# Pooled attention and a two-layer network on one core: the last quarter of group 0's output product is placed among group 1's first hidden products, and the sums of VectorE and GpSimd are re-ordered

## The chip, the core and the metric

The kernel runs on one core of one Trainium2 chip. The metric is device time in microseconds (us), from one launch to its end. The kernel before was timed in 8 runs: median 286.16 us, from 285.38 to 286.41. One further execution was recorded by the hardware profiler, and every duration below is from that one.

## What is computed

Inputs are q, k and v with 8 batches, 8 heads, 576 positions and a head size of 64, and two weight matrices w_in (512 x 2048) and w_out (2048 x 512), all float32. The reference, cut to its core:

```python
k_p = k.reshape(B, H, Sp, 8, D).mean(axis=3)        # 576 rows -> 72
v_p = v.reshape(B, H, Sp, 8, D).mean(axis=3)
scores = scale * np.matmul(q, k_p.transpose(0, 1, 3, 2))
attn = np.exp(scores - np.max(scores, axis=-1, keepdims=True))
attn = attn / (np.sum(attn, axis=-1, keepdims=True) + 1e-09)
x = np.matmul(attn, v_p)                            # -> 4608 tokens x 512
h = x @ w_in
out = (h - np.tanh(h)) @ w_out                      # 4608 x 512
```

## The kernel before

**Groups.** The 4608 tokens are worked in nine groups of 512: groups 0 to 7 are the first 512 positions of one batch each, group 8 is what is left of all batches. For each group there is a hidden product (16 tiles of 128 hidden units, 4 matmuls each), then tanh on ScalarE and the subtraction h - tanh(h) on VectorE into a tile Gt, then an output product with w_out.

**Group 0 is different from the others.** Its output product is a plain one: four token blocks (tb 0 to 3) by four quarters of the hidden units (qd 0 to 3). A step `mlp_o(0, tb, qd)` (matmuls at L593) is four matmuls of 128x512. The quarters are taken in the order of `W2_ORDER`, hidden tiles 0-3, 8-11, 4-7 and 12-15, because w_out (the tile w2b) is loaded in such pieces, by GpSimd's DMA queue, with a cast to 16 bits (`load_w2`, L742). Groups 1 to 8 use seven products of half size instead of eight (L665). These need sums of the quarters of w_out, made once: `w_sum` (L648) into w2s, on VectorE and on GpSimd, and a negated part on ScalarE (L1015).

**Order.** The kernel is scheduled by hand (`manual_schedule`): every engine and every DMA queue takes its instructions strictly in the order in which the program text issues them, and waits where one of them has to wait. What follows in the text behind a waiting instruction of the same engine waits too. `after(a, b)` adds a wait by hand.

**The stretch that the change rewrites** lies between group 0's hidden product and group 1's output product. In the order of the text:

- The loop over hidden tiles 5 to 15 of group 0 (L951), matmuls at L564, subtraction at L577, PSUM banks 0 to 4 in turn.
- `pool_k(1)`: the sums of eight neighbouring rows of k of batch 1. First sum on GpSimd (L247), two loads of w_out (tiles 4-5 and 6-7), second sum on GpSimd (L252), the load of tiles 12-15, last sum on VectorE into kd (L259). Then two `w_sum` pieces on GpSimd, which wait for kd.
- SP's queue: the load of k of batch 2 (`load_k(2)`), which is made to wait for `w2_dmas[3]`, the load of tiles 6-7; then v and, a little later, q of batch 2.
- A loop over 16 steps u (L974), one `mlp_o` each. Between the steps stand batch 1's attention: turning k (L328) and q (L216) on TensorE by a product with the identity, the casts of q on ScalarE (L967, L992), scores (L374) and exp (L389, L406), the sums of v on VectorE (`pool_v(1)`, L270 to L309, in one piece of five tiles), the product with v (L463) and its division (L480, L481), and the turn of the result (L542, L549) into xT, group 1's input. On VectorE stand the `w_sum` pieces besides. The last quarter is steps 12 to 15; after it ScalarE copies each block out (L601) and SP stores it (L681).
- `pool_k(2)`, all three sums on GpSimd, `pool_v(2)` on GpSimd, and one last `w_sum` on VectorE.
- Group 1 (loop over g): seven `h_pair` steps (L608, eight matmuls into two PSUM banks, tanh L621 over both, subtraction L622), whose bank pairs start at 2, 0, 4, 6, 0, 2, 4; two `h_one`; then the seven products, among which stand scores and attention of batch 2 (L422, L448). During p 2 to 4 ScalarE casts q of batch 2 and SP turns it by DMA transposes (L202, L207); SP turns kd of batch 2 (L350), GpSimd places it (`k_place`, L360 to L362), SP spreads v (L293 to L295) and loads k, v and q of batch 3. In the products, SP turns group 2's input by DMA transposes (L527).

A pair of banks can be written again when the subtraction of its `h_pair` has read it:

```python
t2 = TS[:, 2 * ts : 2 * ts + 2, :]
nc.scalar.activation(out=t2, in_=PS[:, b0 : b0 + 2, :], func=ACT.Tanh)
nc.vector.tensor_sub(out=Gt[:, p, :, :], in0=PS[:, b0 : b0 + 2, :], in1=t2)
```

The softmax here doesn't subtract the row's maximum and nothing guards it: scores larger than these inputs give would overflow.

## Time and profile before

| what | us |
|---|---|
| median of 8 runs | 286.16 |
| the profiled execution: its own time | 286.41 |
| its span from first to last instruction | 284.7 |
| TensorE busy | 276.3 |
| VectorE busy | 223.5 |
| ScalarE busy | 157.8 |
| GpSimd busy | 115.1 |
| group 0's hidden product ends | 33.71 |
| group 1's first `h_pair` starts | 54.49 |
| group 1's seven products start | 68.32 |
| group 2's first `h_pair` starts | 84.15 |

The span and the 1.7 us around it make the execution's own time. TensorE is busy for 97% of the span, so it is read by its gaps: the list of waits names each gap and the engine or DMA that ended it. The chain of waits is the chain of work that ended last, followed back from the end of the span; a piece "PE PS L608 x72" in it is 72 matmuls of line 608 one after the other. The granted TensorE clock is full speed from the first slices to the last but one.

### The profile page before, as it was taken

What the parts mean: (1) busy time and instruction counts of PE and PEld (TensorE: products, weight loads), DVE (VectorE), ACT (ScalarE), POOL (GpSimd) and SP (SyncE); (2) the same over time, 40 slices, a digit from 0 to 9 for tenths busy, and PEclk for the clock granted to TensorE, in tenths of its full rate; (3) what the DMA queues carried; (4) which work ended last, traced back from release to release, by engine and by line L of the source; (5) the groups of instructions that cost most, each with busy time, mean ns of one, the idle gap of its engine ahead of it and who ended that gap; (6) DMA issues with size and microseconds to landing.
All of it is one profiled execution on the core that took longest, in us unless ns stands there. A gap on an engine that the chain in (4) does not pass through costs nothing.

```text
span 284.7 us, 5465 instructions
## 1 busy us (share of the span) xinstructions
PE 276.3 (97%) x2156; PEld 180.0 (63%) x2156; DVE 223.5 (78%) x338; ACT 157.8 (55%) x212; POOL 115.1 (40%) x124
## 2 busy tenths in 40 slices
PE   7999989999989999999999999999999999999994
PEld 3454445645874489548954795479547964884583
DVE  6568787989965998599959985998599839946983
ACT  4737567696527571867186708680868156215510
POOL 8600743693398019900990099109910110010000
PEclk9999999999999999999999999999999999999998
DMA  7999998974999894889588966897550440012014
GB/s 248 231 212 275 288 217 230 324 206 94 351 207 184 233 336 88 136 276 335 103 107 273 353 117 115 267 323 145 110 166 0 69 163 0 2 67 83 0 37 113
DMA packets 67253, 50.41 MB, mean 177 GB/s; under 512 B 42652, under 2 KB 56476, under 8 KB 67228
## 3 DMA queue, kind: packets, MB, share of 16 engines
q1 hardware_dynamic: 57724, 36.04, 50.5%
q0 software_dynamic: 6784, 12.06, 17.2%
q10 hardware_dynamic: 2720, 1.97, 2.4%
q8 instruction: 17, 0.28, 0.4%
q14 instruction: 8, 0.07, 0.1%
HBM read 36.70 MB, written 9.44 MB: 162 GB/s over the span
## 4 chain that ended last, share of the span: by engine, by line
PE 91%; DMA 4%; ACT 1%; DVE 1%; issue 1%; SPq 0%; ACTq 0%
PE PS L608 39%; PE PS L665 33%; PE PS L564 5%; PE PS L593 5%; PE PS L422 3%; PE PS L448 3%; DMA xT<-x_sb 2%; DMA k_raw<-in_k_dram 2%; PE PS L463 1%; PE PS L374 1%; ACT qT L132 0%; PE PS L844 0%; PE PS L905 0%; PE PS L216 0%; PE PS L755 0%
## 5 line engine op out<-in xcount | busy, mean ns | idle before, releaser
L608 PE MATMUL PS<-xT,w1b 128*128 128x512 bf16 (+1 forms) x504 | 98.1, 355 | 0.7 <-DMA xT<-x_sb 0.7
L622 DVE TENSOR_TENSOR Gt<-PS,TS 128x1024 bf16<-128x1024 f32 x56 | 68.4, 1221 | 33.2 <-ACT TS L621 33.1
L608 PEld LDWEIGHTS <-w1b 128*128 128x128 f16 x576 | 56.2, 98 | 53.7 <-DMA xT<-x_sb 1.0
L621 ACT ACTIVATE TS<-PS 128x1024 f32<-128x1024 f32 x56 | 57.3, 1024 | 31.0 <-PE PS L608 28.5
L709 POOL TENSOR_TENSOR m<-O,m 128x512 f32<-128x512 f32 x6 | 7.6, 1260 | 76.9 <-ACT m L707 76.9
L665 PE MATMUL PS<-w2s,Dg 128*128 128x256 f16 x256 | 30.2, 272 | 0.0
L247 POOL TENSOR_TENSOR k_raw<-k_raw 128x512 f32<-128x512 f32 (+2 forms) x13 | 21.5, 1672 | 19.1 <-DMA k_raw<-in_k_dram 19.1
L443 ACT ACTIVATE E<-PS 72x1024 bf16<-72x1024 f32 (+1 forms) x30 | 26.1, 929 | 4.0 <-PE PS L422 3.7
L665 PEld LDWEIGHTS <-Gt 128*128 128x128 bf16 x256 | 23.5, 98 | 6.8 <-issue 2.3
L665 PEld LDWEIGHTS <-P 128*128 128x128 bf16 x256 | 24.6, 98 | 3.0
L665 PEld LDWEIGHTS <-Dg 128*128 128x128 bf16 x256 | 24.6, 98 | 2.8
L630 DVE TENSOR_TENSOR P<-Gt 128x1024 bf16<-128x1024 bf16 x32 | 22.0, 687 | 0.6
L716 ACT COPY m<-PS 128x512 f32<-128x512 f32 x8 | 4.7, 586 | 29.6 <-PE PS L665 29.6
L681 POOL DMA_DIRECT2D out_dram<-O x14 | 7.7, 552 | 31.7 <-DVE O L719 29.5
L640 DVE TENSOR_TENSOR Dg<-Gt 128x1024 bf16<-128x1024 bf16 x32 | 20.4, 684 | 0.0
L270 POOL TENSOR_TENSOR v_raw<-v_raw 128x512 f32<-128x512 f32 (+1 forms) x12 | 18.2, 1536 | 0.0
L499 DVE TENSOR_TENSOR x_sb<-PS,rden 128x512 bf16<-128x512 f32 x24 | 16.6, 692 | 0.8
L665 PE MATMUL PS<-w2s,Gt 128*128 128x256 f16 x128 | 16.4, 273 | 0.0
L665 PE MATMUL PS<-w2b,P 128*128 128x256 f16 x128 | 16.3, 273 | 0.0
L665 PE MATMUL PS<-w2b,Gt 128*128 128x256 f16 x128 | 16.3, 272 | 0.0
L665 PE MATMUL PS<-w2s,Q 128*128 128x256 f16 x128 | 16.3, 272 | 0.0
L1090 ACT COPY O<-PS 128x512 f32<-128x512 f32 x7 | 4.1, 586 | 21.9 <-PE PS L665 21.9
(120 smaller groups left out, 405.7 us busy)
## 6 DMA issues: line engine op xcount, KB each, us to landing
k_raw<-in_k_dram SPq DMA_DIRECT2D x7, 1024.0 KB, 6.0
q_raw<-in_q_dram SPq DMA_DIRECT2D x7, 1024.0 KB, 11.3
v_raw<-in_v_dram SPq DMA_DIRECT2D x7, 1024.0 KB, 8.8
out_dram<-O POOLq DMA_DIRECT2D x14, 512.0 KB, 3.8
w1b<-in_moe_w_in_dram POOLq DMA_DIRECT2D x4, 512.0 KB, 14.1
w2b<-in_moe_w_out_dram POOLq DMA_DIRECT2D x3, 512.0 KB, 23.2
out_dram<-O SPq DMA_DIRECT2D x2, 512.0 KB, 7.0
k_raw<-in_k_dram SPq DMA_DIRECT2D x7, 128.0 KB, 6.0
```

Of the source, the lines that this page charges most:

```text
L247: eng.tensor_tensor(out=r[:, ta:tb, 0:4, :], in0=r[:, ta:tb, 0:4, :], in1=r[:, ta:tb, 4:8, :], op=ALU.add)
L270: eng.tensor_tensor(out=r[:, ta:tb, 0:4, :], in0=r[:, ta:tb, 0:4, :], in1=r[:, ta:tb, 4:8, :], op=ALU.add)
L443: nc.scalar.activation(out=e, in_=ps, func=ACT.Exp, scale=SCALE)
L499: nc.vector.tensor_tensor(out=x_sb[:, :, :, :], in0=ps[:, :, :, 0:D], in1=rden[:, :, :, :].to_broadcast([128, 2, 4, D]), op=ALU.mult,)
L564: nc.tensor.matmul(h_tiles[i][:, :], lhsT=w1b[:, fb, i * 128 : (i + 1) * 128], rhs=xT[g][:, :, fb, :], start=(fb == 0), stop=(fb == NFB - 1),)
L593: nc.tensor.matmul(o_ps[:, :], lhsT=gts[i][:, tb * 128 : (tb + 1) * 128], rhs=w2b[:, i, :], start=(i == 0), stop=(i == NHID - 1),)
L608: nc.tensor.matmul(dst[:, t0 * 128 : t1 * 128], lhsT=w1b[:, fb, i * 128 : (i + 1) * 128], rhs=x[:, t0:t1, fb, :], start=(fb == 0), stop=(f ...
L621: nc.scalar.activation(out=t2, in_=PS[:, b0 : b0 + 2, :], func=ACT.Tanh)
L622: nc.vector.tensor_sub(out=Gt[:, p, :, :], in0=PS[:, b0 : b0 + 2, :], in1=t2)
L630: nc.vector.tensor_tensor(out=P[:, a:b, :], in0=Gt[:, a:b, 0, :], in1=Gt[:, a:b, 1, :], op=ALU.add)
L640: return nc.vector.tensor_tensor(out=Dg[:, a:b, :, :], in0=Gt[:, a:b, :, 0:HT], in1=Gt[:, a:b, :, HT:TG], op=ALU.subtract,)
L665: nc.tensor.matmul(part(g, bk, tt), lhsT=lhs(k, slice(tt * 128, (tt + 1) * 128)), rhs=rhs[:, k, :], start=(first and k == 0 and (tt == 0 o ...
```

## The change

- In group 0's loop the sums of the fifth tile of v of batch 1 are made after hidden tile 9 (`pool_v1(NM, NT)`: four instructions on VectorE); the banks of the loop are i % 5 throughout. The load of v of batch 1 is in two halves.
- `pool_k(1)` issues no loads. Behind it on GpSimd's queue stand the two `w_sum` pieces that wait for kd, then one load of w_out's tiles 4-7. The load of tiles 12-15 stands later and is made to wait for the first load of k of batch 2, which in turn waits for `w2_dmas[2]`, now the load of tiles 4-7.
- The 16 steps are written out. Twelve of them (quarters 0 to 2) stay ahead of group 1; attention of batch 1 lies among them, with both halves of the division in one pair of instructions (L499, L500 in the new file) and the sums of v in pieces. Group 0's four PSUM tiles are banks 1, 2, 3 and 0; attention uses banks 4 to 7.
- `pool_k(2)`: first sums on GpSimd, second and last sum on VectorE, where they stand ahead of group 1's subtractions. `pool_v(2)`, two `w_sum` pieces and `k_place(2)` follow on GpSimd.
- Group 1's bank pairs start at 6, 4, 6, 4, 6, 4, 2. Ahead of p 4 stands `rest_of_group_0`: casts and DMA transposes of q of batch 2, the four steps of the last quarter with their copies and stores, three `w_sum` pieces and a sum for group 1 on VectorE, the loads of batch 3 and the spread of v on GpSimd's queue.

The engines' instruction streams otherwise hold the same work: TensorE has the same number of matmuls before and after.

```diff
@@ -237,7 +237,7 @@
     def halves(n, b):
         return ((0, n),) if b < 2 else ((0, n // 2), (n // 2, n))
 
-    def pool_k(b, eng, t0=0, t1=NT, mid=(), last=None, dep2=None):
+    def pool_k(b, eng, t0=0, t1=NT, last=None, second=None):
         r = k_raw[b % 2].rearrange("p t (j d) -> p t j d", d=D)[:, t0:t1, :, :]
         if b not in kdups:
             kdups[b] = work.tile([128, NT, 2, D], BF16, name="kd", tag="kd", bufs=1)
@@ -247,15 +247,9 @@
             eng.tensor_tensor(
                 out=r[:, ta:tb, 0:4, :], in0=r[:, ta:tb, 0:4, :], in1=r[:, ta:tb, 4:8, :], op=ALU.add
             )
-        for i, m in mid[0:2]:
-            load_w2(i, m)
-        second = eng.tensor_tensor(
+        (second or eng).tensor_tensor(
             out=r[:, :, 0:2, :], in0=r[:, :, 0:2, :], in1=r[:, :, 2:4, :], op=ALU.add
         )
-        if dep2 is not None:
-            after([second], dep2)
-        for i, m in mid[2:]:
-            load_w2(i, m)
         kd_done = (last or eng).tensor_tensor(
             out=kd,
             in0=r[:, :, 0:1, :].to_broadcast([128, n, 2, D]),
@@ -273,12 +267,6 @@
         eng.tensor_tensor(
             out=r[:, :, 0:2, :], in0=r[:, :, 0:2, :], in1=r[:, :, 2:4, :], op=ALU.add
         )
-        if b < 2:
-            eng.tensor_tensor(
-                out=r[:, :, 0, :], in0=r[:, :, 0, :], in1=r[:, :, 1, :], op=ALU.add
-            )
-            v_main(VB[b % 2], r[:, :, 0:1, :], eng, 0, NM)
-            return v_left(VB[b % 2], r[:, NM, 0:1, :], eng)
         if b < 4:
             eng.memset(VB[b % 2][0:G, 0:H, D:D1], float(POOL))
         vps[b] = work.tile([128, NT, D], BF16, name="vp", tag="vp", bufs=1)
@@ -286,17 +274,30 @@
             out=vps[b][:, :, :], in0=r[:, :, 0, :], in1=r[:, :, 1, :], op=ALU.add
         )
 
+    def pool_v1(ta, tb):
+        r = v_raw[1].rearrange("p t (j d) -> p t j d", d=D)
+        for n in (4, 2, 1):
+            nc.vector.tensor_tensor(
+                out=r[:, ta:tb, 0:n, :],
+                in0=r[:, ta:tb, 0:n, :],
+                in1=r[:, ta:tb, n : 2 * n, :],
+                op=ALU.add,
+            )
+        if ta == NM:
+            return v_left(VB[1], r[:, NM, 0:1, :], nc.vector)
+        return v_main(VB[1], r[:, :, 0:1, :], nc.vector, ta, tb)
+
     vps = {}
 
-    def v_spread(b):
+    def v_spread(b, eng=nc.sync):
         vp, vb = vps.pop(b), VB[b % 2]
-        nc.sync.dma_start(out=vb[0:G, 0:H:2, 0:D], in_=vp[0:G, 0:NM, :])
-        nc.sync.dma_start(out=vb[0 : 128 - G, 1:H:2, 0:D], in_=vp[G:128, 0:NM, :])
-        nc.sync.dma_start(out=vb[128 - G : G, 1:H:2, 0:D], in_=vp[0 : NM * LO, NM, :])
+        eng.dma_start(out=vb[0:G, 0:H:2, 0:D], in_=vp[0:G, 0:NM, :])
+        eng.dma_start(out=vb[0 : 128 - G, 1:H:2, 0:D], in_=vp[G:128, 0:NM, :])
+        eng.dma_start(out=vb[128 - G : G, 1:H:2, 0:D], in_=vp[0 : NM * LO, NM, :])
 
     def v_main(vb, vs, eng, t0, t1):
         n = t1 - t0
-        eng.tensor_tensor(
+        return eng.tensor_tensor(
             out=vb[:, 2 * t0 : 2 * t1, 0:D].rearrange("p (t s) d -> p t s d", s=2),
             in0=vs[:, t0:t1, :, :].to_broadcast([128, n, 2, D]),
             in1=mask[:, 2 * t0 : 2 * t1, :]
@@ -583,13 +584,12 @@
 
     o_tiles = {}
 
-    def mlp_o(g, tb, qd, gts, pool=None, k0=0, k1=4):
+    def mlp_o(g, tb, qd, gts):
         if qd == 0:
-            p, tag = pool or (ps_o, "o_ps")
-            o_tiles[tb] = p.tile([128, DM], FP32, name="o_ps", tag=tag)
+            o_tiles[tb] = bank((1, 2, 3, 0)[tb], [128, DM])
         o_ps = o_tiles[tb]
         i0 = W2_ORDER[qd]
-        for i in range(i0 + k0, i0 + k1):
+        for i in range(i0, i0 + 4):
             nc.tensor.matmul(
                 o_ps[:, :],
                 lhsT=gts[i][:, tb * 128 : (tb + 1) * 128],
@@ -941,7 +941,8 @@
     ps_h.n = ps_o.n = 0
     nc.scalar.copy(out=q_bf[:QT, R, :, :], in_=t0[:QT, :, R, :])
     load_q(1, False)
-    load_main(v_pairs, v_raw[1], 1, 0, NM)
+    load_main(v_pairs, v_raw[1], 1, 0, 2)
+    load_main(v_pairs, v_raw[1], 1, 2, 4)
     load_q_tail(1, q_raws[1], nc.scalar)
     for i in range(5):
         mlp_h_mms(0, i, 2, 4)
@@ -949,108 +950,132 @@
 
 
     for i in range(5, NHID):
-        mlp_h(0, i, gts, bank((0, 1, 2, 3, 4, 0, 1, 2, 3, 4, 2)[i - 5], [128, TG]))
+        mlp_h(0, i, gts, bank(i % 5, [128, TG]))
         if i == 7:
             q_pe_tail(0)
         if i == 9:
             scores_tail(0)
+        if i == 9:
+            pool_v1(NM, NT)
         if i == 11:
             ps_a.n = 0
             av(0, 4, ps_any, True)
             x_dma_transpose(0, 2)
-    kd1 = pool_k(1, nc.gpsimd, mid=((4, 2), (6, 2), (12, 4)), last=nc.vector)
-    after([w_sum(w2s[:, 3, :, :], b21, b11, ALU.subtract, nc.gpsimd, k, k + 2) for k in (0, 2)], kd1)
-    after(load_k(2), w2_dmas[3])
-    load_v(2)
-
-    def q1_cast(t, h):
+    def q1_cast(h):
         nc.scalar.copy(
             out=q_bf[:, 0:R, h : h + 4, :].rearrange("p j h d -> p h j d"),
-            in_=t[:, h : h + 4, 0:R, :],
-        )
-
-    o_pools = [(ps_o, "o_ps"), (ps_o, "o_ps"), (ps_h, "hT_ps"), (ps_h, "hT_ps")]
-    pend = []
-    for u in range(16):
-        qd, tb = u // 4, u % 4
-        if u == 8:
-            scores_wide(1, (3,))
-            scores_ends(1)
-        if qd == 2:
-            for t2 in (2 * (tb % 2), 2 * (tb % 2) + 1):
-                mlp_o(0, t2, qd, gts, o_pools[t2], tb // 2 * 2, tb // 2 * 2 + 2)
-        else:
-            mlp_o(0, tb, qd, gts, o_pools[tb])
-        if u == 0:
-            q1 = q_raws.pop(1)
-            q1_cast(q1, 0)
-        if u == 3:
-            k_transpose(1, ps_any, (nc.vector.tensor_copy, nc.vector.tensor_copy))
-        if u == 4:
-            q_pe_transpose(1, (0, 1), "act")
-            q1_cast(q1, 4)
-            nc.scalar.copy(out=q_bf[:QT, R, :, :], in_=q1[:QT, :, R, :])
-            load_q(2)
-            w_sum(w2s[:, 1, :, :], b11, b12, ALU.add, k1=4)
-            w_sum(w2s[:, 0, :, :], b11, b22, ALU.add, k1=4)
-            w_sum(w2s[:, 2, :, :], b21, b22, ALU.add, k1=4)
-            w_sum(b12, b22, b12, ALU.subtract, k1=4)
-            v1_done = pool_v(1, nc.vector)
-            after(
-                [
-                    w_sum(w2s[:, 3, :, :], b21, b11, ALU.subtract, nc.gpsimd, k, k + 2)
-                    for k in (4, 6)
-                ],
-                v1_done,
-            )
-            w_sum(w2s[:, 1, :, :], b11, b12, ALU.add, k0=4)
-        if u in (5, 6):
-            q_pe_transpose(1, (u - 3,), "act")
-        if 5 <= u <= 7:
-            scores_wide(1, (u - 5,))
-        if u == 6:
-            q_pe_tail(1)
-        if u in (9, 11):
-            n = (u - 9) // 2
-            nc.scalar.mul(
-                out=w2s[:, 4, 4 * n : 4 * n + 4, :], in_=b22[:, 4 * n : 4 * n + 4, :], mul=-1.0
-            )
-        if 11 <= u <= 14:
-            x_pe_transpose(1, *pend.pop(0))
-        if 9 <= u <= 12:
-            pend.append((u - 9, av(1, u - 9, ps_any, False)))
-        if u == 13:
-            w_sum(w2s[:, 0, :, :], b11, b22, ALU.add, k0=4)
-            sums = w_sum(w2s[:, 2, :, :], b21, b22, ALU.add, k0=4)
-        if u == 15:
-            ps_a.n = 0
-            av(1, 4, ps_any, True)
-    pool_k(2, nc.gpsimd, dep2=sums)
+            in_=q1[:, h : h + 4, 0:R, :],
+        )
+
+    def negated(n):
+        nc.scalar.mul(
+            out=w2s[:, 4, 4 * n : 4 * n + 4, :], in_=b22[:, 4 * n : 4 * n + 4, :], mul=-1.0
+        )
+
+    def turn1(blk):
+        x_pe_transpose(1, blk, x_pairs[1, blk // 2][:, blk % 2])
+
+    ps_a = Banks(4, 5, 6, 7)
+    q1 = q_raws.pop(1)
+    kd1 = pool_k(1, nc.gpsimd, last=nc.vector)
+    after([w_sum(w2s[:, 3, :, :], b21, b11, ALU.subtract, nc.gpsimd, k, k + 2) for k in (0, 2)], kd1)
+    load_w2(4, 4)
+    w_sum(w2s[:, 1, :, :], b11, b12, ALU.add, k1=4)
+    mlp_o(0, 0, 0, gts)
+    q1_cast(0)
+    q1_cast(4)
+    nc.scalar.copy(out=q_bf[:QT, R, :, :], in_=q1[:QT, :, R, :])
+    mlp_o(0, 1, 0, gts)
+    mlp_o(0, 2, 0, gts)
+    k_transpose(1, ps_any, (nc.vector.tensor_copy, nc.vector.tensor_copy))
+    w_sum(w2s[:, 0, :, :], b11, b22, ALU.add, k1=4)
+    w_sum(w2s[:, 2, :, :], b21, b22, ALU.add, k1=4)
+    mlp_o(0, 3, 0, gts)
+    mlp_o(0, 0, 1, gts)
+    q_pe_transpose(1, (0, 1), "act")
+    pool_v1(0, 2)
+    mlp_o(0, 1, 1, gts)
+    scores_wide(1, (0,))
+    q_pe_transpose(1, (2,), "act")
+    w_sum(b12, b22, b12, ALU.subtract, k1=4)
+    pool_v1(2, 4)
+    mlp_o(0, 2, 1, gts)
+    scores_wide(1, (1,))
+    q_pe_transpose(1, (3,), "act")
+    q_pe_tail(1)
+    mlp_o(0, 3, 1, gts)
+    scores_wide(1, (2, 3))
+    scores_ends(1)
+    negated(0)
+    w_sum(w2s[:, 1, :, :], b11, b12, ALU.add, k0=4)
+    mlp_o(0, 0, 2, gts)
+    ps_a.n = 0
+    k2 = load_k(2)
+    after(k2, w2_dmas[2])
+    load_v(2)
+    load_q(2)
+    load_w2(12, 4)
+    after([w2_dmas[3]], k2[0])
+    av(1, 0, ps_any, True)
+    av(1, 1, ps_any, True)
+    mlp_o(0, 1, 2, gts)
+    turn1(0)
+    mlp_o(0, 2, 2, gts)
+    turn1(1)
+    av(1, 2, ps_any, True)
+    av(1, 3, ps_any, True)
+    mlp_o(0, 3, 2, gts)
+    turn1(2)
+    turn1(3)
+    av(1, 4, ps_any, True)
+    pool_k(2, nc.gpsimd, last=nc.vector, second=nc.vector)
+    x_pairs.pop((1, 0))
+    x_pairs.pop((1, 1))
+    k_dma_transpose(2)
+    x_dma_transpose(1, 2)
     pool_v(2, nc.gpsimd)
-    w_sum(b12, b22, b12, ALU.subtract, k0=4)
+    for k in (4, 6):
+        w_sum(w2s[:, 3, :, :], b21, b11, ALU.subtract, nc.gpsimd, k, k + 2)
+    k_place(2, nc.gpsimd.tensor_copy)
+
+    def rest_of_group_0():
+        for n in range(3):
+            q_cast_part(2, n)
+            q_dma_transpose(2, n)
+        for tb in range(4):
+            mlp_o(0, tb, 3, gts)
+        w_sum(w2s[:, 0, :, :], b11, b22, ALU.add, k0=4)
+        w_sum(w2s[:, 2, :, :], b21, b22, ALU.add, k0=4)
+        sum_p(2, 4)
+        w_sum(b12, b22, b12, ALU.subtract, k0=4)
+        load_k(3)
+        load_v(3)
+        load_q(3)
+        v_spread(2, nc.gpsimd)
 
     for g in range(1, NG):
         nb = g + 1 if g + 1 < B else None
         nn = g + 2 if g + 2 < B else None
         for p in range(NP - 1):
-            c = p if g > 1 else p - 2
-            if nb is not None and 0 <= c < 3:
-                q_cast_part(nb, c)
-            h_pair(g, p, ((2, 0, 4, 6, 0, 2, 4) if g == 1 else (0, 2, 4, 6, 0, 2, 4))[p], p % 2)
-            if 3 <= p < 6:
+            if g == 1 and p == 4:
+                rest_of_group_0()
+            if nb is not None and g > 1 and p < 3:
+                q_cast_part(nb, p)
+            h_pair(g, p, ((6, 4, 6, 4, 6, 4, 2) if g == 1 else (0, 2, 4, 6, 0, 2, 4))[p], p % 2)
+            if g == 1 and p == 2:
+                negated(1)
+            if 3 <= p < 6 and (g > 1 or p != 4):
                 sum_p(2 * p - 6, 2 * p - 4)
-            if nb is not None and p == 0:
+            if nb is not None and g > 1 and p == 0:
                 k_dma_transpose(nb)
-            if g == 1 and p == 0:
-                x_dma_transpose(1, 2)
             if g > 1 and p == 0:
                 store(g - 1, 2, 4, nc.gpsimd)
                 store(g - 1, 0, 2, nc.gpsimd)
-            if nb is not None and p == 0:
+            if nb is not None and g > 1 and p == 0:
                 k_place(nb, nc.gpsimd.tensor_copy)
-            if nb is not None and 0 <= c < 3:
-                q_dma_transpose(nb, c)
-            if nb is not None and c == 2:
+            if nb is not None and g > 1 and p < 3:
+                q_dma_transpose(nb, p)
+            if nb is not None and g > 1 and p == 2:
                 v_spread(nb)
                 if nn is not None:
                     load_k(nn)
@@ -1064,7 +1089,7 @@
         if nb is not None:
             sum_d(0, 2)
             sum_d(2, 4)
-        ps_a = Banks(2, 3, 4, 5, 0, 1)
+        ps_a = Banks(*((4, 5, 2, 3, 0, 1) if g == 1 else (2, 3, 4, 5, 0, 1)))
         for u in range(14):
             n, half = u // 2, u % 2
             bk, lhs, rhs = products[n]
```

## The prediction

> **What bounds the kernel now.** I read the share of busy time first, then TensorE's waits, then the chain of waits in order of time. TensorE's list of waits for the whole span:
>
> ```profile
> PE PS L755 <- DVE xT_last L767: 1.3, 1, 1.3
> PE PS L216 <- ACT q_bf L967: 1.0, 1, 1.0
> PE PS L608 <- DMA xT<-x_sb: 0.7, 1, 0.7
> ...
> ```
>
> Two gaps only lie behind the kernel's start: 1.0 us in group 0's output product, where TensorE waits for the second cast of q, and 0.7 us at the head of group 2. The chain of waits (start, us, what) shows the same places:
>
> ```profile
> 39.64 0.95 ACT q_bf L967
> ...
> 54.49 13.83 PE PS L608 x72
> ...
> 77.61 6.49 DMA xT<-x_sb
> ...
> ```
>
> All else from 33.71 on is matmuls back to back, and the change leaves their number alone. So the change can gain 1.02 + 0.74 = 1.76 us at most, and anything that makes TensorE wait is a loss in full. The question is whether the new order keeps it fed. For that I read GpSimd's timeline (start, us, line, tile), since the loads of weights and the first sums of k go through it:
>
> ```profile
> 29.96 2.90 POOL L247 TENSOR_TENSOR k_raw<-k_raw 128x1280 f32<-128x1280 f32 x1 [16.17 <-DMA k_raw<-in_k_dram]
> 32.80 1.46 POOL L742 DMA_DIRECT2D w2b<-in_moe_w_out_dram  x2
> 34.27 1.56 POOL L252 TENSOR_TENSOR k_raw<-k_raw 128x640 f32<-128x640 f32 x1
> 35.76 0.78 POOL L742 DMA_DIRECT2D w2b<-in_moe_w_out_dram  x1
> 36.78 2.26 POOL L648 TENSOR_TENSOR w2s<-w2b 128x512 f16<-128x512 f16 x2 [0.24 <-DVE kd L259]
> 46.42 2.27 POOL L648 TENSOR_TENSOR w2s<-w2b 128x512 f16<-128x512 f16 x2 [7.38 <-DMA w2b<-in_moe_w_out_dram]
> 51.63 3.48 POOL L247 TENSOR_TENSOR k_raw<-k_raw 128x512 f32<-128x512 f32 x2 [2.93 <-DMA k_raw<-in_k_dram]
> ```
>
> Tiles 4 to 7 of w_out are asked for at 32.8. SP's queue shows the load of k of batch 2 released by them at 44.43; its sums begin at 51.63.
>
> **Step 1: the head of the stretch (gain 1.02).** Both casts of q now stand ahead of everything else on ScalarE, so the wait at L216 goes. Next late would be ScalarE itself: casts from 36.49 (when q lands) for 0.95 + 0.95 + 0.55 (their spacing in its timeline), free at about 39.0. TensorE comes to the transposes of q at 38.3, and their copies, two of 0.59, are first needed by the scores at 39.65, after one more `mlp_o`. Hidden, within 0.1. Attention gets four banks in turn instead of three; by the same spacing I find no bank that is late. The stretch from 33.71 to 54.49 is 20.78; without the gap and without the last quarter (16 matmuls, 3.46, paid later) it is 16.30, so group 1 could start at 50.0. Quarter qd 2 began at 44.87 and would begin at 43.85.
>
> **Step 2: tiles 4 to 7 of w_out come later (cost about 1.15).** Their load now stands on GpSimd behind both k sums and both `w_sum` pieces, and those wait for kd. GpSimd: 29.96 + 2.90 + 1.56 = 34.4; kd on VectorE follows the last subtraction (it ended at 35.07), so 35.05 + 0.83 = 35.9; `w_sum` 2.26 to 38.25; issue 0.75 to 39.0. When does it land? The trace has no such load on a quiet queue, so I bound it. In 42.0 to 44.5 the software queue alone moved 0.49 MB, 0.2 MB per us, so 512 KB need 2.6 us. Early end: the 512 KB stores on the same queue land 3.8 us after issue (median); plain data move about twice as fast (395 GB/s in the window 35.2 to 36.4), so 1.2 more, 38.25 + 5.0 = 43.3. Late end: in 35.2 to 36.4 that queue moved nothing, though two loads had been issued by 34.26, so a load can start some 3 us after its issue; the load of tiles 12-15 had its bytes through by 44.5 and landed at 46.4, 1.9 later: 39.0 + 3.0 + 2.6 + 1.9 = 46.5. I take the middle, 45.0, since the two nearest rows differ in kind (a store without a cast) and in crowding. TensorE then waits 1.15 before qd 2.
>
> The Trainium skill, "DMA: Bandwidth & Descriptors", section "Anatomy of one DMA — SWDGE (gpsimd) path", gives 2.0 us plus bytes over 436 GB/s: 3.2 us as an estimate, so a landing at 41.45, no wait here, and, by the last part of step 3, a time of 285.3. The trace's 10.0 and 10.5 us for these loads, in a crowd, are far from it.
>
> From the start of qd 2 to group 1 it is 6.15 (50.0 - 43.85), and 0.25 more as group 1's first banks, 6 and 7, have just held the last turned blocks, which ScalarE copies out: start at 51.4.
>
> **Step 3: k of batch 2 blocks VectorE's queue (cost about 4.2).** The load of k waits for tiles 4-7 as before it waited for tiles 6-7, so it is issued at 45.0, not earlier than the old 44.43. Behind it now comes a longer row of waits: GpSimd waits for its landing, issues the load of tiles 12-15, and only then makes the first sums; VectorE makes the second and the last sum, *ahead of group 1's subtractions in its queue*. DMA issues of this load and GpSimd's sums at batch 3:
>
> ```profile
> k_raw<-in_k_dram SPq DMA_DIRECT2D x1, 1024.0 KB, 7.1
> ```
>
> ```profile
> 77.09 3.04 POOL L247 TENSOR_TENSOR k_raw<-k_raw 128x512 f32<-128x512 f32 x2
> ```
>
> Landing 6.0 (5.8 for batch 3, 7.1 here, where other loads were still running), issue 0.78, first sums 3.05, second sum 0.83 (L273 has its shape on VectorE), last sum 0.83, the subtraction of pair 0 1.22, semaphores 0.1. One thing more: VectorE and GpSimd shut each other out when both read two tiles from SBUF. VectorE's timeline:
>
> ```profile
> 52.08 3.58 DVE L648 TENSOR_TENSOR w2s<-w2b 128x1024 f16<-128x1024 f16 x2
> ```
>
> Two `w_sum` that take 0.68 each elsewhere take 3.58 while GpSimd sums k. GpSimd goes on with v of batch 2, which lands about then (8.3 to 9.5 us after issue), so its first v sum, 1.27 (59.26 in its timeline), falls between VectorE's second and last sum. Together 14.1: the subtraction of pair 0 ends at 59.1. Without the v sum and with 5.8 it is 12.6; with two v sums (1.27 and 1.8), 7.1 and 3.48 it is 17.4.
>
> Who waits: pairs 0 and 1 run from 51.4 to 54.9; pair 2 needs banks 6 and 7, which pair 0's subtraction frees. Even with VectorE free it would wait 0.65, as a pair's end to the end of its subtraction takes 2.4 (tanh 1.02, subtraction 1.22, hand-overs) against 1.73 for a pair. With the k sums it waits until 59.1, 4.2 us. After that there is pairs 2 to 6, the two singles and the last quarter: 6 x 1.73 + 3.46 = 13.84, so the seven products start at 72.9 instead of 68.32: **+4.6**. What lies beside it: the load of tiles 12-15 (issued at about 51.5, sharing the engines with v and q; wanted at 62.6), the rest of GpSimd's list (done near 65), q's casts and transposes (near 71, wanted at 73.8). VectorE has 3.3 us of sums behind the last quarter; if GpSimd holds it up there, the products wait up to 1.2; I take 0, since GpSimd is through by then.
>
> **Step 4: the gap at group 2 goes (gain 0.74).** The DMA transposes that end it stood in SP's ring behind q of batch 3, issued at 71.22 and 11.3 to 11.6 us on its way. The new order issues the loads of batch 3 at about the same clock time, after the copies of the last quarter, but group 2 starts some 4 us later. If the loads come later by as much, the gap stays.
>
> Nothing: dividing both halves at once (VectorE is not late there), v's spread on GpSimd's queue, v's halves, the moved `w_sum` pieces.
>
> **The sum.** 286.41 + 4.6 - 0.74 = 290.3 for an execution like the profiled one; that lay 0.25 above the median, so **290.1**. In short: 286.2 plus (landing of tiles 4-7 minus 41.1).
>
> **Rivals.**
> *The collision at 29.96 (slower still, 292.9).* VectorE now sums v's fifth tile after its subtraction that ends at 29.02: by the rows for 256 and 128 columns 0.42 and 0.29, by their slope 0.23 for 64, so the fourth instruction begins at about 30.05, and GpSimd's k sum begins at 29.96 and holds for 2.9. If GpSimd comes first, VectorE stands until 32.9, six subtractions and kd come 2.8 late, and with kd the load of tiles 4-7: +2.8. For: the margin is 0.1 us. Against: the same 0.1 us.
> *k in time (faster, 285.3).* If tiles 4-7 land by 41.5, k's sums are through when pair 0's tanh is: first sums done by 51.35, k landed by 47.5. Then only 0.65 + 0.25 is lost against 1.76: -0.9. For: the old loads were in a crowd of v, a DMA transpose and each other. Against: GpSimd isn't free to issue before 38.25, and 3.2 us would be less than any 512 KB load here took.
> *Near no change (286.3).* Tiles 4-7 land between 41 and 42 and k's chain is as I have it: the losses eat the gain.
>
> **Chances.** Forecast 0.45; collision 0.30; slower still, by 17.4 for the chain or VectorE late before the products, 0.08; k in time 0.10; near no change 0.07. Faster by over 0.2% 0.10, within it 0.07, slower 0.83; 0.2% is about what a measurement of this kernel can tell from no change. The forecast's own range: 43.3 and 12.6 give 286.9, 46.5 and 14.1 give 291.6; the collision at 46.5 gives 294.4. With the two cases at the low end and part of the last left out: 287.0 to 294.4.
>
> **What would show it.** TensorE's waits list "DMA w2b" of about 1 us before the third quarter, and one of about 4 us at L608 for VectorE, in the third pair; VectorE waits for GpSimd's k sum ahead of group 1; no wait at the casts of q; the products start near 73 and group 2 without a gap. The collision shows as a VectorE instruction of about 3 us near 30. I am wrong if GpSimd's load issue comes before 37, or if the k sums end before pair 0's tanh.

## The result and the profile after

The changed kernel is **slower**: its 11 timed executions have a median of 295.92 us (290.45 to 297.16), against 285.69 us (284.96 to 287.32, 32 executions) of the kernel before on the same chips. The ratio of the two is 1.0233, interval 1.0202 to 1.0264, which on the 286.16 us of the start is some 292.8 us. The ratio leaves out every execution more than 1.5% above the fastest of its kernel, which is more than half of the changed kernel's, so both numbers are given: the loss is 2.3% in its better executions and some 3.6% by the medians of all.

The profiled execution took 297.71 us with a span of 295.9 us: 11.2 us more than the span before. TensorE's list of waits answers the one shown above (line waited for: total us, times, longest):

```profile
PE PS L608 <- DVE Gt L622: 6.2, 1, 6.2
PE PS L593 <- DMA w2b<-in_moe_w_out_dram: 1.5, 1, 1.5
...
PE PS L565 <- DVE Gt L578: 0.9, 1, 0.9
PE PS L329 <- DVE kd L253: 0.8, 2, 0.6
```

The wait for the second cast of q is gone. In its place stand 6.2 us at L608, 1.5 us for w_out, and 1.5 us that VectorE causes earlier (0.9 at L565 and 0.6 of the 0.8 at L329; the rest of that lies at the kernel's start). The chain of waits (start, us, what; its short pieces named "issue" and "DVEq" are left out) shows how they hang together:

```profile
29.98 3.02 DVE VB L310
...
38.24 3.11 POOL w2s L648 x2
41.35 5.56 DMA w2b<-in_moe_w_out_dram
46.92 5.42 DMA k_raw<-in_k_dram
52.88 0.74 POOL w2b L742
53.64 3.04 POOL k_raw L247 x2
56.71 3.64 DVE k_raw L250
60.38 2.04 DVE kd L253
62.41 1.15 DVE Gt L622
63.60 5.92 PE PS L608 x16
```

Between 29.98 and 63.60, in this chain, TensorE does not lead: VectorE, GpSimd and two transfers follow one another, and TensorE waits for whichever is late. The seven products start at 79.88, against 68.32 before. Three things are to be seen here that the forecast's sum has not, or not at this size.

VectorE's timeline (start, us, line, tile) and GpSimd's carry the first two:

```profile
29.98 3.02 DVE L310 TENSOR_TENSOR VB<-v_raw,mask 128x256 bf16<-128x256 f32 x1
...
56.71 3.63 DVE L250 TENSOR_TENSOR k_raw<-k_raw 128x640 f32<-128x640 f32 x1 [1.88 <-POOL k_raw L247]
60.38 2.04 DVE L253 TENSOR_TENSOR kd<-k_raw 128x640 bf16<-128x640 f32 x1
```

```profile
29.83 2.89 POOL L247 TENSOR_TENSOR k_raw<-k_raw 128x1280 f32<-128x1280 f32 x1 [16.49 <-DMA k_raw<-in_k_dram]
...
56.64 3.01 POOL L264 TENSOR_TENSOR v_raw<-v_raw 128x512 f32<-128x512 f32 x2
59.73 2.00 POOL L267 TENSOR_TENSOR v_raw<-v_raw 128x640 f32<-128x640 f32 x1
```

**The collision at 29.96 took place.** The fourth instruction for v's fifth tile takes 0.43 us when it is alone (run e1 below) and 3.02 here: it came 0.15 us after GpSimd's k sum and ends 0.28 us behind it (33.00 and 32.72). Everything behind it on VectorE is late, kd too, and GpSimd stands idle for 3.84 us until kd is there, so the load of tiles 4 to 7 is issued at 41.35 (39.04 in e1).

**VectorE's sums of k cost 5.7 us, not 2.9.** The second sum of k begins at 56.71, 0.07 us after GpSimd has begun the first of its two v sums (56.64), and lasts until *both* are over (59.65) and 0.7 us longer. GpSimd's next sum then overlaps its end, and VectorE's last sum (2.04) overlaps that one. That these lengths are waiting is what run e8 below shows: with GpSimd's v sums out of the way the two take 0.83 and 0.82.

**TensorE's clock fell by half during the wait.** Sixteen matmuls of L608 take 3.46 us before and 5.92 here. Windows of the changed kernel (stretch, length, busy time and instructions of PE, PEld, DVE, ACT and POOL; then the granted clock, DMA share and GB/s):

```profile
60.00:63.00 3.00, 0.00 (x0) 0.00 (x0) 2.97 (x3) 0.00 (x0) 2.99 (x3) 0.74 0.80 148
63.00:66.00 3.00, 2.40 (x6) 0.84 (x6) 1.68 (x2) 0.00 (x0) 2.80 (x5) 0.50 0.40 78
66.00:69.00 3.00, 3.00 (x10) 1.13 (x9) 0.74 (x1) 1.79 (x2) 2.42 (x5) 0.62 0.12 22
```

TensorE stops at 57.4; from about 61.4 to 68.3 the clock is 0.50, so the first 4.7 us of work after the wait run at half speed. In the kernel before, whose longest wait behind the start is 1.0 us, no such stretch exists.

### The profile page after: what moved, and what is told of

It reads as the page before. It is cut to its first block, busy times and chain, and to the rows that moved or that the text cites. A ratio compares the mean times of both kernels' runs of the same rounds, so it can differ in the third digit from the quotient of the medians.

```text
span 295.9 us, 5460 instructions
## 1 busy us (share of the span) xinstructions
PE 279.3 (94%) x2156; PEld 180.5 (61%) x2156; DVE 228.9 (77%) x339; ACT 157.8 (53%) x212; POOL 113.1 (38%) x124
## 4 chain that ended last, share of the span: by engine, by line
PE 79%; DMA 8%; DVE 7%; POOL 2%; issue 1%; ACT 1%; SPq 0%; DVEq 0%; POOLq 0%
PE PS L608 37%; PE PS L665 31%; DMA k_raw<-in_k_dram 4%; PE PS L565 3%; PE PS L423 3%; PE PS L449 2%; DMA w2b<-in_moe_w_out_dram 2%; DMA xT<-x_sb 2%; DVE k_raw L250 1%; DVE Gt L578 1%; PE PS L593 1%; DVE kd L253 1%; POOL w2s L648 1%; POOL k_raw L247 1%; DVE VB L310 1%
## 5 line engine op out<-in xcount | busy, mean ns | idle before, releaser
L608 PE MATMUL PS<-xT,w1b 128*128 128x512 bf16 (+1 forms) x504 | 100.8, 361 | 6.7 <-DVE Gt L622 6.2
L622 DVE TENSOR_TENSOR Gt<-PS,TS 128x1024 bf16<-128x1024 f32 x56 | 68.3, 1221 | 37.7 <-ACT TS L621 37.7
L608 PEld LDWEIGHTS <-w1b 128*128 128x128 f16 x576 | 56.8, 99 | 61.6 <-issue 10.3
L665 PE MATMUL PS<-w2s,Dg 128*128 128x256 f16 x256 | 30.2, 272 | 0.0
L665 PEld LDWEIGHTS <-Gt 128*128 128x128 bf16 x256 | 23.6, 98 | 7.0 <-issue 2.5
L665 PEld LDWEIGHTS <-P 128*128 128x128 bf16 x256 | 24.5, 98 | 3.0
L665 PEld LDWEIGHTS <-Dg 128*128 128x128 bf16 x256 | 24.6, 98 | 2.8
L500 DVE TENSOR_TENSOR x_sb<-PS,rden 128x512 bf16<-128x512 f32 x28 | 19.4, 692 | 1.0
L593 PE MATMUL PS<-w2b,Gt 128*128 128x512 f16 x64 | 15.6, 379 | 1.7 <-DMA w2b<-in_moe_w_out_dram 1.5
L665 PE MATMUL PS<-w2s,Gt 128*128 128x256 f16 x128 | 16.4, 273 | 0.0
L665 PE MATMUL PS<-w2b,P 128*128 128x256 f16 x128 | 16.3, 273 | 0.0
L665 PE MATMUL PS<-w2b,Gt 128*128 128x256 f16 x128 | 16.3, 272 | 0.0
L665 PE MATMUL PS<-w2s,Q 128*128 128x256 f16 x128 | 16.3, 272 | 0.0
```

The lines of the kernel that those rows point to most:

```text
L500: nc.vector.tensor_tensor(out=x_sb[:, :, :, :], in0=ps[:, :, :, 0:D], in1=rden[:, :, :, :].to_broadcast([128, 2, 4, D]), op=ALU.mult,)
L593: nc.tensor.matmul(o_ps[:, :], lhsT=gts[i][:, tb * 128 : (tb + 1) * 128], rhs=w2b[:, i, :], start=(i == 0), stop=(i == NHID - 1),)
L608: nc.tensor.matmul(dst[:, t0 * 128 : t1 * 128], lhsT=w1b[:, fb, i * 128 : (i + 1) * 128], rhs=x[:, t0:t1, fb, :], start=(fb == 0), stop=(f ...
L665: nc.tensor.matmul(part(g, bk, tt), lhsT=lhs(k, slice(tt * 128, (tt + 1) * 128)), rhs=rhs[:, k, :], start=(first and k == 0 and (tt == 0 o ...
```

## The experiments

The theory after the result (A): the loss is a sum of separate causes, the collision at 29.98, the k sums on VectorE with their exclusion, and the late loads of w_out; take one away and its price comes back. The rival (B): these causes cover each other; behind each the next transfer or engine is late, so the wait moves. All kernels but the last were compared with the kernel before in five rounds; ratios are to it.

### e1: the sums of v's fifth tile two hidden tiles earlier

```diff
-        if i == 9:
+        if i == 7:
             pool_v1(NM, NT)
```

> The changed kernel with one edit: the sums of v's fifth tile stand after hidden tile 7 instead of 9, two microseconds earlier on VectorE, so GpSimd's first k sum (29.8) can't shut them out. Theory A (four losses in a row: collision, late load of w_out tiles 4-7, k sums ahead of the subtractions on VectorE, and a lower clock after the long wait): the VectorE instruction of 3.0 us at L310 shrinks to 0.43, kd ends near 35.9 instead of 38.15, the load of tiles 4-7 is issued near 38.3 instead of 41.35, everything behind comes 2.5 to 3 us earlier; the wait of 6.2 in the third pair stays. Ratio to before 1.011 to 1.018 where the change had 1.023. Rival B (the collision only uses up time that TensorE would spend waiting for k anyway): same ratio as the change, 1.02 or more.

Measured: 1.0198 [1.0160, 1.0236], median 291.84 us (290.55 to 295.33). VectorE's fourth instruction for v, GpSimd's load of tiles 4 to 7, and TensorE's third pair:

```profile
29.12 0.43 DVE L310 TENSOR_TENSOR VB<-v_raw,mask 128x256 bf16<-128x256 f32 x1
...
39.04 0.79 POOL L742 DMA_DIRECT2D w2b<-in_moe_w_out_dram  x1
...
61.49 5.12 PE L608 MATMUL PS<-xT,w1b 128*128 128x512 bf16 x16 [6.33 <-DVE Gt L622]
```

The collision is gone, the load is issued at 39.04 instead of 41.35 and lands at 44.69 instead of 46.92. The third quarter starts 2.2 us earlier and the products at 76.97 instead of 79.88, 2.9 us in the trace; 4.1 us by the medians of all executions, but only 0.3% by the ratios, whose intervals overlap (1.0160 to 1.0236 here, 1.0202 to 1.0264 there): by them alone, the rival can't be told from a gain. In the trace the collision costs a little over 2 us on its own, and the larger part of the loss is elsewhere: the wait in front of the third pair is still 6.33 us, with the same 3.63 and 2.04 on VectorE, and the 16 matmuls after it take 5.12.

### e2: all three sums of k of batch 2 on GpSimd

```diff
-    pool_k(2, nc.gpsimd, last=nc.vector, second=nc.vector)
+    pool_k(2, nc.gpsimd)
```

> The changed kernel with one edit: the second and last k sum of batch 2 go back to GpSimd, so that group 1's subtractions wait for nothing on VectorE's queue. Theory A: the third pair waits 0.65 us (two pairs of banks) instead of 6.2, the clock stays at full speed, the products start 7 to 8 us earlier than 79.9: near 72; collision and late load stay. Ratio to before 0.998 to 1.006. Rival B (the blocked queue is only the first of several late things, and the k chain comes to TensorE another way, by the last quarter's weights or by kT): the wait moves to L593 or L423, ratio 1.012 or more.

Measured: 1.0269 [1.0242, 1.0297], median 293.81 us. The wait of 6.2 us shrinks to 0.7, as theory A wants; of the time little follows, as the rival wants: 2.1 us by the medians of all executions, while the ratio is even above the changed kernel's 1.0233 (what the ratio leaves out is said with the result). TensorE's timeline where group 2 begins:

```profile
91.29 8.99 PE L608 MATMUL PS<-xT,w1b 128*128 128x256 bf16 x41 [2.37 <-DMA xT<-x_sb]
```

The last quarter now comes 6 us sooner, though it stands 2.04 us for tiles 12 to 15, which were issued at 52.56 behind the landing of k. The products begin at 73.91, 6.0 us ahead of the changed kernel, and group 2 then waits 2.37 us for the DMA transposes of its input, which stand in SP's ring behind the loads of batch 3. After those 2.37 us the clock is near half again (the window's seventh column, 0.53):

```profile
92.00:94.00 2.00, 2.00 (x13) 1.44 (x11) 0.00 (x0) 0.00 (x0) 1.91 (x4) 0.53 0.48 93
```

Group 2's 72 matmuls take 15.68 us instead of 13.83. With the wait of 2.37 that uses up most of the 6.0 us: the span is 293.4, 2.5 below that of the changed kernel. The collision took place here too (3.14 us at L310), and in e3 (3.04).

### e3: the load of tiles 4 to 7 between the two k sums of batch 1

```diff
+        if mid:
+            load_w2(*mid)
         (second or eng).tensor_tensor(
...
-    kd1 = pool_k(1, nc.gpsimd, last=nc.vector)
+    kd1 = pool_k(1, nc.gpsimd, last=nc.vector, mid=(4, 4))
...
-    load_w2(4, 4)
```

> The changed kernel with one edit: the load of w_out tiles 4-7 is issued between the first two k sums of batch 1, as the kernel before issued them, and not behind the two pieces that wait for kd. Theory A: issued near 32.8, landed between 40 and 42.5, so no wait ahead of the third quarter (1.5 gone), k of batch 2 asked for 4.5 to 6 us earlier and its sums nearly through when pair 0's tanh is: the wait of 6.2 falls to between 1 and 2.5, no lower clock. Ratio 1.000 to 1.010. Rival B (the load takes some 10 us when it shares the rings, as before): landing near 44, the k chain stays late, ratio 1.012 or more.

Measured: 1.0195 [1.0155, 1.0235], median 292.08 us: above the range that was expected, since the load's place was worth less. It is issued 8.3 us earlier (33.00) and lands 3.9 us earlier (43.0): 10.0 us on its way, against 5.6 on a quieter queue. No wait for w_out is left ahead of the third quarter, but VectorE's sums of k still hold the third pair for 3.14 us, and the 16 matmuls take 5.08.

### e4: the three edits together

> All three edits together. Theory A: none of the waits is left but 0.65 for the two pairs of banks and some 0.25 at group 1's head, against 1.02 and 0.74 that the kernel before has: ratio 0.996 to 0.999, 284.6 to 285.6 us. Rival B (another loss hides behind these): ratio 1.003 or more, with a wait that none of the other three shows.

Measured: 1.0142 [1.0116, 1.0167], median 290.28 us. The rival was right: with all three edits 1.4% of loss stays. One named cause was not taken away, for the load of tiles 4 to 7 lands no earlier than in e1. TensorE at the last quarter of group 0:

```profile
61.72 3.61 PE L595 MATMUL PS<-w2b,Gt 128*128 128x512 f16 x16 [1.81 <-DMA w2b<-in_moe_w_out_dram]
```

Most of the rest is waits for transfers: 1.30 us for tiles 4 to 7, which were issued at 32.79 and land only at 45.1 (12.3 us on their way), and 1.81 for tiles 12 to 15. VectorE causes 1.2 more, 0.7 at L610 and 0.5 at L425. The clock stays at full speed after 1.81 us: 16 matmuls take 3.61 in this view, as in the other rows at full clock (3.61 or 3.62).

### e5: both loads of w_out early, and batch 3's ahead of the last quarter

```diff
     q1 = q_raws.pop(1)
+    load_w2(4, 4)
     kd1 = pool_k(1, nc.gpsimd, last=nc.vector)
+    load_w2(12, 4)
...
-    load_w2(4, 4)
...
-    load_w2(12, 4)
-    after([w2_dmas[3]], k2[0])
...
     def rest_of_group_0():
+        load_k(3)
+        load_v(3)
```

The edits of e1 and e2 are in it too, and q of batch 3 is loaded ahead of the last quarter.

> All three edits, and besides: the load of w_out tiles 4-7 is issued ahead of the first k sum of batch 1 (near 14, GpSimd being idle), the load of tiles 12-15 right behind the second k sum (near 34.5) without waiting for k of batch 2, and the loads of batch 3 ahead of the last quarter. Theory A2 (the three edits still left 1.3 and 1.8 us of waits for w_out, since the loads are what binds the stretch; 0.7 for the two pairs of banks remains): no wait for w_out at L593, group 1 starts near 50.3, the products near 68.2, group 2 without a gap: ratio 0.995 to 0.999. Rival B2 (w_out ahead of v and q on the DMA rings makes those late instead): new waits at the casts of q, at kd or at v's sums, ratio 1.002 or more.

Measured: 1.0167 [1.0146, 1.0187], median 290.75 us. As the rival expected, no wait for w_out is left, and two others came in, 1.6 us for the casts of q at L216 and 1.9 us in the products (L665). q of batch 1 lands at 39.05 now (ScalarE waited 4.50 us for it), and an output tile in the products is held up by a store that is late; VectorE's timeline there:

```profile
79.55 0.69 DVE L703 TENSOR_TENSOR O<-PS,m 128x512 f32<-128x512 f32 x1 [3.07 <-DMA out_dram<-O]
```

In the stretch 54 to 58 of the kernel before, the busy share of the DMA engines is 1.12 already. Here what was moved ahead came with others that are late.

### e6: the kernel before with q's three casts first (step 1 alone)

```diff
             q1_cast(q1, 0)
+            q1_cast(q1, 4)
+            nc.scalar.copy(out=q_bf[:QT, R, :, :], in_=q1[:QT, :, R, :])
...
-            q1_cast(q1, 4)
-            nc.scalar.copy(out=q_bf[:QT, R, :, :], in_=q1[:QT, :, R, :])
```

> The kernel before with one edit: all three casts of q of batch 1 stand one behind the other ahead of the other work of ScalarE, as in the changed kernel. It does alone what step 1 of the prediction priced at 1.02 us. As recorded (the gap is a gain in full): 1.0 us, ratio 0.9965. Theory A2 (the gap covers the landing of tiles 6-7 at 44.4, needed at 43.85 without it): the wait at L216 goes, one of 0.4 to 0.6 for w_out comes at the third quarter, gain 0.4 to 0.6, ratio 0.998 to 0.9986.

Measured: 0.9990 [0.9970, 1.0010], median 285.59 us of 12. The wait at L216 for the second cast is gone. In the profiled execution, which was this kernel's slowest (288.42 us), other waits stand in its place: 1.4 us at L608 and 0.5 us at L422, both for VectorE, and this one:

```profile
PE PS L593 <- DMA w2b<-in_moe_w_out_dram: 0.6, 1, 0.6
```

It is for tiles 4 and 5 of w_out, which land some 3 us later than before, at 45.1. The issue of their load, in the window 32 to 33.45, first before, then here (size, us to landing):

```profile
w2b<-in_moe_w_out_dram POOLq DMA_DIRECT2D x1, 256.0 KB, 9.1
```

```profile
w2b<-in_moe_w_out_dram POOLq DMA_DIRECT2D x1, 256.0 KB, 11.8
```

The load of tiles 6 and 7 ends at 46.5 instead of 44.4, and behind it on SP's queue k, v and q of batch 2 are asked for later. ScalarE waits for that q, between two tanh of group 1:

```profile
61.87 1.04 ACT L184 CAST q_bf<-q_raw 128x1024 bf16<-128x1024 f32 x1 [2.03 <-DMA q_raw<-in_q_dram]
```

So its third tanh comes at 62.82 instead of 59.91, VectorE's third subtraction at 63.87 instead of 60.97, and group 1's last eight matmuls wait 1.4 us. Theory A2 had the place of the wait for w_out right, but not its reason. In the trace before, tiles 4 and 5 landed at 41.9, 3.0 us ahead of their first matmul, and tiles 6 and 7 at 44.4, 2.5 us ahead of theirs (46.95): the gap of 1.02 was not what covered them. Why the loads take longer here is not shown.

### e7: the wait filled with work

This is e1 with 28 matmuls of zeros added to an open sum just ahead of the third pair; the sums keep their values.

```diff
+            if g == 1 and p == 2:
+                for _ in range(28):
+                    nc.tensor.matmul(
+                        o_tiles[3][:, :],
+                        lhsT=zeros[:, 0:128],
+                        rhs=zeros[:, 0:512],
+                        start=False,
+                        stop=False,
+                        skip_group_check=True,
+                    )
             h_pair(g, p, ((6, 4, 6, 4, 6, 4, 2) if g == 1 else (0, 2, 4, 6, 0, 2, 4))[p], p % 2)
```

> The changed kernel with v's fifth tile after hidden tile 7, and 28 matmuls of zeros (6.05 us, added onto an open sum) in the place where TensorE waits for the third pair's banks. Useful work is the same. Theory C (after a wait of more than 2.4 us TensorE is granted half its clock for some 3.5 us): the 16 matmuls behind the wait take 3.46 instead of 5.12, no 5 or 6 in the row of granted clocks, ratio 1.012 to 1.016 where the same kernel without the zeros had 1.0198. Rival (the slow stretch comes from what VectorE and GpSimd do then, not from the wait): they stay slow, ratio 1.019 or more.

Measured: 1.0266 [1.0235, 1.0297], median 292.9 us. TensorE's timeline:

```profile
54.30 6.21 PE L1066 MATMUL PS<-xT_last 128*128 128x512 bf16 x28
60.35 3.62 PE L608 MATMUL PS<-xT,w1b 128*128 128x512 bf16 x16
```

The clock theory is right in the row that it speaks of: with no idle time ahead of them the same 16 matmuls take 3.62 instead of 5.12, and the mean granted clock is 1.0 in five of six executions. The time is no better, since here the zeros outlasted what they fill: pair 0's subtraction was over at 57.7, and the third pair had to queue until 60.35. In this execution the exclusion fell a milder way, which the edit did not aim at: VectorE's second sum began at 53.95, ahead of GpSimd's first v sum at 54.14, and its two sums took 0.83 and 1.78.

### e8: GpSimd's v sums wait until VectorE has kd

This is e1 with one wait more.

```diff
-    pool_k(2, nc.gpsimd, last=nc.vector, second=nc.vector)
+    kd2 = pool_k(2, nc.gpsimd, last=nc.vector, second=nc.vector)
...
-    pool_v(2, nc.gpsimd)
+    pool_v(2, nc.gpsimd, dep=kd2)
```

> The changed kernel with v's fifth tile after hidden tile 7, and GpSimd's v sums of batch 2 made to wait for kd, so that VectorE's two k sums run with GpSimd at rest. Theory D (VectorE and GpSimd shut each other out): these two take 0.83 each instead of 3.63 and 2.04, the third pair starts 3.5 to 4 us earlier, its wait falls from 6.3 to 2.3 to 2.8, and the slow clock shrinks or goes; ratio 1.003 to 1.009. Rival (they are slow for another reason): same durations, ratio 1.018 or more.

Measured: 1.0156 [1.0128, 1.0183], median 290.26 us. VectorE, and TensorE's third pair:

```profile
53.91 0.83 DVE L250 TENSOR_TENSOR k_raw<-k_raw 128x640 f32<-128x640 f32 x1 [2.25 <-POOL k_raw L247]
54.77 0.82 DVE L253 TENSOR_TENSOR kd<-k_raw 128x640 bf16<-128x640 f32 x1
...
56.78 5.30 PE L611 MATMUL PS<-xT,w1b 128*128 128x512 bf16 x16 [2.57 <-DVE Gt L625]
```

3.63 and 2.04 are 0.83 and 0.82 with the v sums out of the way, and the wait at the third pair falls from 6.33 to 2.57 us: the exclusion is shown, at 4.0 us. The ratio falls less than expected. One reason is in the trace: the clock still drops after 2.57 us (the 16 matmuls take 5.30). It can't be the only one: three of the six executions have a mean granted clock of 1.0, so no drop, and take 288.69 to 291.08 us, against 290.11 to 291.53 for the others.

### e9 and e10: steps 4 and 1 on the kernel before

e9 puts the spread of v of batch 2 on GpSimd's queue, so that the loads of batch 3 leave SP earlier (q at 67.32 instead of 71.22); e10 has e6's edit besides.

```diff
-                v_spread(nb)
+                v_spread(nb, nc.gpsimd if g == 1 else nc.sync)
```

> The kernel before with one edit: v of batch 2 is spread from GpSimd's queue, so that on SP's queue the loads of batch 3 stand right behind the transposes of q and are issued some 2.7 us earlier (near 66 instead of 68.7). Theory A2 (the gap of 0.74 at group 2 is DMA transposes behind the load of q of batch 3): the gap goes, 0.5 to 0.74 us, ratio 0.9974 to 0.9985. Rival (the spread of v now lands late, or the earlier loads delay the transposes of batch 2): a wait at L448 or L422, ratio 1.000 or more.

> The kernel before with both edits, the casts of q first and the loads of batch 3 earlier: all that the new order could win, without the new order. Theory A2: the gains add, 0.4 + 0.7, ratio 0.995 to 0.9975. Rival: they don't add, 0.998 or more.

Measured: e9 0.9997 [0.9982, 1.0011], median 285.78; e10 0.9987 [0.9969, 1.0004], median 285.59 (12 executions each). In e9's profile the 0.7 us at the head of group 2 is gone, but a wait of 0.4 us for VectorE stands in the scores of the products; e10 has 0.6 and 0.5 us for VectorE and 0.4 for w_out, whose tiles 4 and 5 are 11.8 us on their way as in e6. Neither gain can be measured: in the traces, waits of about half the size came in where the two gaps were closed.

### e11: e4, with tiles 12 to 15 loaded right behind tiles 4 to 7

```diff
     kd1 = pool_k(1, nc.gpsimd, last=nc.vector, mid=(4, 4))
+    load_w2(12, 4)
...
-    load_w2(12, 4)
-    after([w2_dmas[3]], k2[0])
```

> All three edits of the changed kernel, and the load of w_out tiles 12-15 right behind the second k sum of batch 1 (near 34.5) instead of behind the landing of k of batch 2. Theory A2: the wait of 1.8 at the last quarter goes and nothing takes its place (k of batch 2 comes later, but no longer holds VectorE): ratio 1.006 to 1.010 where all three edits alone had 1.014. Rival B2 (the DMA rings are full, so what is moved forward makes another transfer late by as much): a new wait of 1 us or more, ratio 1.012 or more.

Measured: 1.0075 [1.0053, 1.0097], median 287.92 us, the best of the kernels with the new order. The wait of 1.81 us is gone, so the load's hand-made wait for k of batch 2 had cost about that, 0.7% by the ratios. The ratio lies in theory A2's range, but it is not true that nothing came in: the wait at L425 grew from 0.5 to 1.5 us. What is left:

```profile
PE PS L425 <- DVE Gt L624: 1.5, 1, 1.5
...
PE PS L595 <- DMA w2b<-in_moe_w_out_dram: 1.2, 1, 1.2
PE PS L610 <- DVE Gt L624: 0.7, 1, 0.7
```

These three, 3.4 us, take the place of the 1.7 that the kernel before had.

### e12: the changed kernel once more

> The changed kernel itself once more, for a second look at the two encounters of VectorE and GpSimd (at 29.98 and behind 56.7), which hang on some 0.1 us and on when v lands. Theory D: the four fixed places are the same (casts without a wait, a wait for tiles 4-7 near 45, the third pair's wait for VectorE, a slow clock behind it), and the two encounters may fall otherwise; times spread over 290 to 297 as before. If both fall the same way and the time is the same within 0.3 us, they are no chance.

Measured: median 297.24 us of 6 (291.19 to 298.18). Its profile tells the same story as the first one. VectorE's instruction at L310 takes 3.00 us (at 29.91), and the sums of k take 3.63 and 2.04 (from 56.85). The 16 matmuls after the wait (6.24 us) take 6.49 this time. So the drop's price differs from one execution to the next, 5.92 and 6.49 for the same work. Both encounters fell the same way, and the time (297.87) is within 0.2 us of the first profiled one: by what was set down ahead, that is no chance, for executions of this length. The one of 291.19 left no trace.

## Why the prediction was right, and where its sizes were not

The sign and the range held: 292.8 by the ratio lies in 287.0 to 294.4. It is the size of the rival "collision at 29.96" (292.9), and that collision did happen; but the agreement is in part luck. The 292.8 stands for executions of which none left a trace; the two that did took 297.71 and 297.87, above the range, as is the median of all, 295.92. In those two, a term of the sum was mis-sized and one was missing. By the prediction's own marks on the time line, for the profiled executions (starts of work that directly followed other work are 0.17 earlier in a timeline than in the chain; here as in the chain):

| mark | predicted | e1 (no collision) | changed kernel |
|---|---|---|---|
| TensorE free for the third quarter | 43.85 | 43.92 | 45.44 |
| tiles 4-7 landed, third quarter starts | 45.0 | 44.7 | 46.95 |
| group 1 starts | 51.4 | 51.6 | 53.9 |
| pair 0's subtraction ends, third pair starts | 59.1 | 61.5 | 63.6 |
| products start | 72.9 | 76.97 | 79.88 |
| span | 288.6 | 292.3 | 295.9 |

**Step 1 (gain 1.02): right in its row, worth nothing measurable alone.** In e1 TensorE is free at 43.92, where 43.85 was forecast. Two things make up this agreement: group 0's hidden product ended 0.58 later than before (34.29), and from there to the third quarter it was 9.63 us instead of the 10.14 forecast. On the old order the edit gave 0.9990 [0.9970, 1.0010] (e6); in its trace the loads landed later, and waits took the gap's place.

**Step 2 (landing at 45.0, wait 1.15): right where its premise held.** In e1 the load is issued at 39.04 and lands at 44.69, wait 0.8. In the changed kernel the load is issued 2.3 us later through the collision, and lands at 46.92; the bound of 46.5 was for a load issued on time. The estimate of 3.2 us from the Trainium skill ("DMA: Bandwidth & Descriptors", section "Anatomy of one DMA — SWDGE (gpsimd) path") does not fit these loads: 5.6 us on a quieter queue, 10.0 and 12.3 in the crowd. With it falls the rival "k in time".

**The collision (chance 0.30): it was the case in both profiled executions**, and in the traces of e2 and e3, which leave v's sums where the change put them. Priced at 2.8, it delays the landing of tiles 4 to 7 by 2.2 us against e1, and the products by 2.9, of which 0.8 is a longer spell at the lower clock. A margin of 0.1 us was as near as the rows could say; VectorE came at 29.98 and GpSimd's sum at 29.83.

**Step 3 (+4.6 at the products): right mechanism, and the step that failed in size.** The terms for the landing of k (6.0 forecast; 5.4 measured, and 0.5 more until GpSimd's next instruction), the issue (0.78; 0.74), the first sums (3.05; 3.04) and the subtraction (1.22; 1.15) held. The term of the exclusion, one v sum of 1.27 us, measured 4.0: 3.63 + 2.04 with it, 0.83 + 0.82 without (e8). The prediction let GpSimd's v sum fall between VectorE's two; instead both v sums ran ahead of VectorE's second sum and a third came ahead of its last. From the landing of tiles 4-7 to the subtraction it was 16.6 us instead of 14.1. The prediction's case of 17.4, with two v sums in the way, comes near it; it had a part of a chance of 0.08, and the range took in only some of it.

**Not in the prediction: the clock.** From the third pair to the products it is 16.3 us instead of 13.84 (15.5 in e1). No row of the kernel before has a wait this long behind its start, and no step asked what a wait of 4 us does to the matmuls after it. e7 shows that it is the idle time: filled, the 16 matmuls take 3.62. This account is for the traced executions; e8 warns against taking the clock's price for that of all.

**Step 4 (gain 0.74): held in e1, not in the changed kernel.** In e1 no wait is left at the head of group 2; in the changed kernel 0.5 is. The doubt that the prediction set down, that the loads of batch 3 come later with all else, was right: k of batch 3 is issued at 76.64 instead of 68.68.

**The sum.** Products at 72.9 forecast, 79.88 measured: the 7.0 between them are 2.0 (collision, as a later landing), 2.5 (exclusion) and 2.4 (clock), to 0.1. In the span 0.4 is added, about what is left of the gap of step 4 (0.5).

What stays open: the executions of the changed kernel spread from 290.45 to 298.18 us, and only two near the upper end left a trace. Whether the collision and the exclusion fall milder in the shorter ones, as the exclusion does in e7, was not seen. It is also open why the same load of w_out takes 5.6 us in one kernel and 12.3 in another. No version here beats the kernel before by more than its interval.

## What to carry to other kernels

Small gaps in a kernel that is 97% busy may not be worth their length: closing two, of 1.02 and 0.74 us, gave 0.9987 [0.9969, 1.0004] (e10), with waits of 0.4 to 0.6 us in their place. Work that VectorE must do ahead of the instructions TensorE waits for is better priced with its exclusion by GpSimd at the worst order, with all sums that stand back to back on GpSimd's queue, and not with one instruction. And a wait of TensorE of more than some 2 us is priced with the slower matmuls behind it.
